# Spectral pairs every fifth step, and the order of two turns in one queue

## The chip, the cores and the metric

The kernel runs on one core of one Trainium2 chip. The metric is the device time of one execution in microseconds (us). A core has five engines that run beside one another and meet at semaphores: TensorE (PE in the profile; its weight loads are PEld), VectorE (DVE), ScalarE (ACT), GpSimd (POOL) and SyncE (SP). SyncE and GpSimd here mostly issue transfers (DMAs), which move data between the core's memory and DRAM on their own. Each engine works through its instructions in the order in which the program was written.

## What is computed

Two operators in a row. The first mixes along the sequence in frequency space: for each of 8 batches of 3008 x 256 numbers a real Fourier transform along the 3008 positions, a product with a complex filter, and the inverse transform. The second is a two-layer perceptron with a PReLU between, on the 24064 rows of 256 that come out.

```python
def _attn_ref(x, filt_r, filt_i):          # x: 8 x 3008 x 256
    X = np.fft.rfft(x, axis=1)
    F = (filt_r + 1j * filt_i)[None, :, :]
    return np.fft.irfft(X * F, n=x.shape[1], axis=1).astype(np.float32)

def _moe_ref(x, w_in, w_out, alpha):       # x: 24064 x 256, w_in: 256 x 2048
    h = x @ w_in
    g = np.maximum(h, 0.0) + alpha * np.minimum(h, 0.0)
    return (g @ w_out).astype(np.float32)
```

## The kernel before

The transform of length 3008 = 47 x 64 is done as matrix products in four stages, each cut into small pieces (class `Fft`, one object for each batch `b`).

- `piece_a` (16 for a batch): one matmul (L168) over the 47 long axis, evicted by `evict` (`on_act`, line 250) into `asb`. After every fourth piece `save_a` (L173) writes a quarter of `asb` to the scratch array `a_dram`; `load_x` then loads the next batch's quarter through GpSimd's queue (L123).
- `turn_a` (L180): four DMAs read `a_dram` back, turned, into `at`. They need the last `save_a` landed.
- `piece_b` (12, called spectral pairs here, two frequencies k1 each): two matmuls (L188) from `at` into a PSUM bank, then two DVE products with the filter, `uu` (L191) and `ww` (L192). `piece_c` (12): four matmuls (L220 reads `uu`, L221 reads `ww`), evicted into `v`.
- `turn_c(q)` (L230): after every third pair four DMAs write a quarter of `v` to `v_dram`. With the last quarter, q = 3, four more (L236) read all of `v_dram` back, turned, into `zt`. These need the writes landed. This is the inverse turn.
- `piece_d` (16): four matmuls (L243) from `zt`, evicted into `yT`, the perceptron's input. Pieces 0 to 3 give the first 752 of a batch's 3008 columns.

`asb`, `at`, `v` and `zt` have one buffer each; the banks `psF` for the pieces two, `uu` and `ww` two each, the output tile `osb` three.

The perceptron runs over blocks of tokens, twelve for each two batches: five of 512, one of 384, six of 512 (`sizes`). A block has 16 steps. In a step j, `up(j)` does two matmuls (L332) into half of `hps`; on odd j the whole of `hps` is evicted by ACT (L337) into `gt`, and DVE does the PReLU with two L340 and one L341. In the same step `prev.down(j)` does a sixteenth of the second product of the block before (L350: four matmuls, or three over the 384 block). When two groups of 128 tokens are complete, ACT evicts them into `osb` (L355) and SyncE stores them (L316).

So there are 768 steps, 96 for each batch, numbered by `step` through the whole run. The Fourier pieces are hung on these steps by a plan written out by hand: `plan_fft(b, a0, ga, ta, b0, gap, d0)` puts `piece_a(i)` on step a0 + ga i, `turn_a` on step ta, `piece_b(kp)` on b0 + gap kp, `piece_c(kp)` three steps later, `turn_c(q)` on b0 + gap (3q + 2) + 4, and `piece_d` from d0 on, the first five on successive steps and the others on every second one. Within a step come `up`, then `down`, then the pieces, those of an earlier batch first. For batches 3 to 7 the arguments are given from p = 96 (b - 1), 96 steps before the batch's own tokens are needed by `up`; batch 2 has p = 96 with a row of its own.

All of `save_a`, `turn_a`, `turn_c` and the stores go through SyncE's one queue, in the order of the steps, and an issue that has to wait holds up the ones behind it. The next batch plans its `piece_a` from p + 42 to p + 72 of the batch at hand, so its `turn_a` falls near the last `turn_c` of that batch.

Of the kernel before, what the change touches and what calls it, by code (L numbers as in the profile page):

```python
# [66 lines left out]
def kernel(  # L67
# [52 lines left out]
    def load_x(b, c):  # L120
        xs = p_x.tile([2 * N1, 8 * D], FP16, name="xs")
        for h in range(2):
            nc.gpsimd.dma_start(out=xs[h * N1 : h * N1 + N1], in_=xrow(b, h, c))  # L123
        return xs
# [236 lines left out]
    def put(step, fn, *args):  # L361
        plan.setdefault(step, []).append((fn, args))

    def plan_fft(b, a0, ga, ta, b0, gap, d0):
        f = Fft(b)
        for i in range(16):
            put(a0 + ga * i, f.piece_a, i, on_act)
        for c in range(4):
            put(a0 + ga * (4 * c + 3), f.save_a, c)
            if b + 1 < NB:  # L370
                put(a0 + ga * (4 * c + 3) + 1,
                    lambda b=b, c=c: xc.update({(b + 1, c): load_x(b + 1, c)}))
        put(ta, f.turn_a, nc.sync)
        for kp in range(12):
            put(b0 + gap * kp, f.piece_b, kp)
            put(b0 + gap * kp + 3, f.piece_c, kp, on_act)
        for q in range(4):
            put(b0 + gap * (3 * q + 2) + 4, f.turn_c, q)
        for i in range(16):
            put(d0 + min(i, 4) + 2 * max(i - 4, 0), f.piece_d, i, on_act)  # L380

    for i in range(4, 16):
        put(i - 4, f0.piece_d, i, both[i % 2])
    plan_fft(1, 10, 1, 26, 40, 3, 91)
    plan_fft(2, 50, 2, 82, 104, 6, 187)
    for b in range(3, NB):
        p = 96 * (b - 1)
        plan_fft(b, p - 54, 2, p - 20, p + 8, 6, p + 91)

    prev = None  # L390
    step = 0
# [43 lines left out]
```

## Time and profile before

| what | value |
|---|---|
| runs shown | 888.08, 890.47, 891.27 us, median 890.47 |
| the profiled execution | 890.82 us |
| its span, first to last instruction | 889.0 us |
| mean granted clock of TensorE | 0.966 |
| ScalarE busy | 587.4 us |
| DMA, mean over the span | 108 GB/s |

A row of the groups by line reads: line, engine, operation, what is written from what, shapes, count; then busy time and mean duration (ns); then the idle time of the engine just before, and what ended it. A row of the timeline has its start, its length, the engine, the line, and in brackets the idle time before it and what ended that. Matmuls are pipelined, so a matmul's length overlaps the next one's; the distance of two starts is what PE spends. A row of waits names who waited for whom: total, times, longest. A row of the windows gives a stretch, its length, then busy time of PE, PEld, DVE, ACT and POOL, and behind these the granted clock, the share of the DMA engines and the rate in GB/s. "SPq" is SyncE's queue of issues; the length there is the time the issuing took.

### The profile page before, as it was taken

What the parts mean: (1) busy time and instruction counts of PE and PEld (TensorE: products, weight loads), DVE (VectorE), ACT (ScalarE), POOL (GpSimd) and SP (SyncE); (2) the same over time, 40 slices, a digit from 0 to 9 for tenths busy, and PEclk for the clock granted to TensorE, in tenths of its full rate; (3) what the DMA queues carried; (4) which work ended last, traced back from release to release, by engine and by line L of the source; (5) the groups of instructions that cost most, each with busy time, mean ns of one, the idle gap of its engine ahead of it and who ended that gap; (6) DMA issues with size and microseconds to landing.
All of it is one profiled execution on the core that took longest, in us unless ns stands there. A gap on an engine that the chain in (4) does not pass through costs nothing.

```text
span 889.0 us, 15377 instructions
## 1 busy us (share of the span) xinstructions
PE 806.8 (91%) x5809; PEld 548.3 (62%) x5809; DVE 612.1 (69%) x1361; ACT 587.4 (66%) x817; POOL 41.3 (5%) x85
## 2 busy tenths in 40 slices
PE   3568899989997999979997999969999899999997
PEld 1234566757664766657664776647666577776665
DVE  2347577668774787748875687748877578877774
ACT  2137667767874768657784768748687576677663
POOL 4102000000000001000010000000000000000000
PEclk9979999989998999989998999989999899999999
DMA  9988916842566136832358224681336422241111
GB/s 213 248 181 172 197 39 134 202 87 56 126 135 158 27 70 131 164 107 49 89 121 184 63 55 94 148 178 31 72 94 129 116 49 54 54 126 31 41 40 52
DMA packets 95378, 95.95 MB, mean 108 GB/s; under 512 B 8312, under 2 KB 85128, under 8 KB 95176
## 3 DMA queue, kind: packets, MB, share of 16 engines
q1 hardware_dynamic: 85448, 78.19, 34.9%
q0 software_dynamic: 8256, 16.00, 12.1%
q10 hardware_dynamic: 1600, 0.79, 0.5%
q8 instruction: 45, 0.74, 0.3%
q14 instruction: 29, 0.24, 0.1%
HBM read 59.55 MB, written 49.81 MB: 123 GB/s over the span
## 4 chain that ended last, share of the span: by engine, by line
PE 81%; DMA 10%; issue 4%; SPq 2%; ACT 2%; POOL 0%; DVE 0%; POOLq 0%; ACTq 0%; DVEq 0%
PE op L350 34%; PE hps L332 34%; PE psF L168 3%; DMA v_dram<-v 3%; PE psF L243 2%; DMA zt<-v_dram 2%; PE psF L220 2%; PE psF L221 2%; PE psF L188 2%; DMA at<-a_dram 2%; DMA a_dram<-asb 2%; DMA xs<-in_x_dram 1%; SPq L230 1%; ACT gt L337 1%; PE hps L168 0%
## 5 line engine op out<-in xcount | busy, mean ns | idle before, releaser
L337 ACT ACTIVATE gt<-hps 128x1024 f16<-128x1024 f32 (+1 forms) x384 | 385.2, 1003 | 149.4 <-PE hps L332 148.1
L332 PE MATMUL hps<-yT,win_s 128*128 128x512 f16 (+1 forms) x1536 | 460.6, 382 | 0.1
L350 PE MATMUL op<-wout_s,gt 128*128 128x256 f16 x3008 | 457.9, 275 | 0.6 <-DVE gt L341 0.6
L350 PEld LDWEIGHTS <-gt 128*128 128x128 f16 x3008 | 296.8, 99 | 195.7 <-issue 8.8
L340 DVE TENSOR_SCALAR m<-gt,alm_s 128x512 f16<-128x512 f16 (+1 forms) x768 | 233.7, 346 | 197.0 <-ACT gt L337 196.5
L341 DVE TENSOR_TENSOR gt<-gt,m 128x1024 f16<-128x1024 f16 (+1 forms) x384 | 261.7, 681 | 21.8
L332 PEld LDWEIGHTS <-win_s 128*128 128x128 f16 x1536 | 146.7, 100 | 31.2 <-issue 5.3
L250 ACT ACTIVATE asb<-psF 96x512 f16<-96x512 f32 x120 | 70.9, 594 | 48.9 <-PE psF L168 48.9
L250 ACT ACTIVATE yT<-psF 128x376 f16<-128x376 f32 x120 | 57.9, 483 | 55.1 <-PE psF L243 54.7
L243 PE MATMUL psF<-wi_s,zt 96*128 96x94 f16 x504 | 45.6, 218 | 40.1 <-DMA zt<-v_dram 38.5
L243 PEld LDWEIGHTS <-zt 96*128 96x128 f16 x512 | 38.6, 106 | 50.5 <-DMA zt<-v_dram 40.2
L191 DVE TENSOR_TENSOR uu<-psF,filt_s 128x512 f16<-128x512 f32 x84 | 57.4, 684 | 5.8 <-PE psF L188 5.8
L355 ACT ACTIVATE osb<-op 128x512 f32<-128x512 f32 x96 | 56.1, 584 | 7.0 <-PE op L350 3.7
L168 PE MATMUL psF<-xs,wf_s 94*96 94x512 f16 x120 | 48.5, 404 | 11.0 <-DMA xs<-in_x_dram 8.9
L192 DVE TENSOR_TENSOR ww<-psF,filts_s 128x512 f16<-128x512 f32 x84 | 57.2, 681 | 0.0
L123 POOL DMA_DIRECT2D xs<-in_x_dram x64 | 32.8, 520 | 475.4 <-PE psF L168 474.3
L250 ACT ACTIVATE v<-psF 128x512 f16<-128x512 f32 x84 | 50.2, 597 | 3.9 <-PE psF L221 3.6
L220 PE MATMUL psF<-uu,twi_s 128*128 128x256 f16 x168 | 41.5, 274 | 0.0
L221 PE MATMUL psF<-ww,twi_s 128*128 128x256 f16 x168 | 41.3, 273 | 0.0
L188 PE MATMUL psF<-at,twf_s 128*128 128x256 f16 x168 | 32.3, 274 | 7.2 <-issue 7.2
L250 ACT ACTIVATE v<-op 128x512 f16<-128x512 f32 x12 | 7.2, 597 | 32.4 <-PE op L221 32.4
L168 PEld LDWEIGHTS <-wf_s 94*96 94x96 f16 x128 | 16.6, 133 | 15.1 <-issue 11.7
(35 smaller groups left out, 134.2 us busy)
## 6 DMA issues: line engine op xcount, KB each, us to landing
out_dram<-osb SPq DMA_DIRECT2D x128, 128.0 KB
a_dram<-asb SPq DMA_DIRECT2D x32, 384.0 KB
v_dram<-v SPq DMA_DIRECT2D x128, 96.0 KB
zt<-v_dram SPq DMA_DIRECT2D x32, 384.0 KB
xs<-in_x_dram POOLq DMA_DIRECT2D x64, 188.0 KB, 5.0
at<-a_dram SPq DMA_DIRECT2D x28, 384.0 KB
twi_s<-c_twi SPq DMA_DIRECT2D x2, 768.0 KB
filts_s<-filt_s SPq DMA_DIRECT2D x2, 768.0 KB
```

Of the source, the lines that this page charges most:

```text
L168: nc.tensor.matmul(ps[0:96], wf1_s, xs[:, o : o + 512], start=True, stop=True)
L191: nc.vector.tensor_mul(uu, px, filt_s[:, 2 * kp : 2 * kp + 2])
L192: nc.vector.tensor_mul(ww, px, filts_s[:, 2 * kp : 2 * kp + 2])
L220: nc.tensor.matmul(pv[:, kh], twi_s[:, k1, 0], uu[:, kh], start=True, stop=False)
L221: nc.tensor.matmul(pv[:, kh], twi_s[:, k1, 1], ww[:, kh], start=False, stop=True)
L243: nc.tensor.matmul(ps[:, m], self.zt[:, 8 * g + 4 * mh + m, dh * 128 : dh * 128 + 128], wi3_s, start=True, stop=True)
L250: nc.scalar.activation(o, i, AF.Copy)
L332: nc.tensor.matmul(self.hps[:, j % 2, 0:tn], win_s[:, kt, j * 128 : (j + 1) * 128], yT[:, kt, self.t0 : self.t0 + tn], start=(kt == 0), st ...
L337: nc.scalar.activation(g[:, :, 0:tn], self.hps[:, :, 0:tn], AF.Copy)
L340: nc.vector.tensor_scalar(m[:, i, 0:tn], g[:, i, 0:tn], 0.0, a, OP.min, OP.mult)
L341: nc.vector.tensor_add(g[:, :, 0:tn], g[:, :, 0:tn], m[:, :, 0:tn])
L350: nc.tensor.matmul(self.op[:, si % 2], self.gts[k][:, 128 * si : 128 * si + 128], wout_s[:, k], start=(k == 0), stop=(k == 15))
```

## The change

Only arguments of `plan_fft` are changed.

```diff
-    plan_fft(1, 10, 1, 26, 40, 3, 91)
-    plan_fft(2, 50, 2, 82, 104, 6, 187)
+    plan_fft(1, 10, 1, 26, 40, 3, 92)
+    plan_fft(2, 50, 2, 86, 104, 5, 187)
     for b in range(3, NB):
         p = 96 * (b - 1)
-        plan_fft(b, p - 54, 2, p - 20, p + 8, 6, p + 91)
+        plan_fft(b, p - 54, 2, p - 22, p + 6, 5, p + 91)
```

In steps counted from p, for batches 3 to 7:

| piece | before | after |
|---|---|---|
| `turn_a` of this batch | p - 20 | p - 22 |
| `turn_a` of the next batch | p + 76 | p + 74 |
| `piece_b` | p + 8, 14, 20 ... 74 | p + 6, 11, 16 ... 61 |
| `piece_c` | p + 11, 17 ... 77 | p + 9, 14 ... 64 |
| `turn_c` 0 to 3 | p + 24, 42, 60, 78 | p + 20, 35, 50, 65 |
| `piece_d` | p + 91 ... 117 | the same |

For batch 2 (p = 96) the pairs start at step 104 with a gap of 5 instead of 6, so `turn_c(3)` is on step 163 instead of 174; its `turn_a` goes from step 82 to 86. Batch 1 keeps all but `piece_d`, which begins on step 92 instead of 91. No instruction is added, removed or changed in size.

## The prediction

> **What bounds the kernel now.** I read the page first, then what TensorE (PE) waits for, then SyncE's queue around one of these waits, then the granted clock behind it.
>
> ```profile
> span 889.0 us, 15377 instructions
> PE 806.8 (91%) x5809; PEld 548.3 (62%) x5809; DVE 612.1 (69%) x1361; ACT 587.4 (66%) x817; POOL 41.3 (5%) x85
> L340 DVE TENSOR_SCALAR m<-gt,alm_s 128x512 f16<-128x512 f16 (+1 forms) x768 | 233.7, 346 | 197.0 <-ACT gt L337 196.5
> L250 ACT ACTIVATE yT<-psF 128x376 f16<-128x376 f32 x120 | 57.9, 483 | 55.1 <-PE psF L243 54.7
> L243 PE MATMUL psF<-wi_s,zt 96*128 96x94 f16 x504 | 45.6, 218 | 40.1 <-DMA zt<-v_dram 38.5
> ```
>
> PE is busy for 806.8 of 889.0 us, so 82.2 us of idle PE are all that a reordering can win. Half of it, 40.1 us, stands before `piece_d` (L243), and 38.5 of that wait for `zt`, which `turn_c(3)` reads back from `v_dram`. One of the six waits is batch 0's, at 62 us, where nothing changes. The waits of PE between 200 and 720 us give the rest in one row:
>
> ```profile
> PE psF L243 <- DMA zt<-v_dram: 30.3, 5, 7.5
> ```
>
> It is the only row of that answer: from 200 to 720 us PE waits for nothing but `zt`, five times, before `piece_d(0)` of batches 2 to 6, 30.3 us in all. Why `zt` is late stands in SyncE's queue, here before batch 4's wait:
>
> ```profile
> 465.68 0.52 SPq L173 DMA_DIRECT2D a_dram<-asb  x1
> 471.19 3.67 SPq L180 DMA_DIRECT2D at<-a_dram  x4
> 474.95 3.86 SPq L230 DMA_DIRECT2D v_dram<-v  x4
> 483.23 1.72 SPq L236 DMA_DIRECT2D zt<-v_dram  x4
> ...
> 487.27 0.50 PE L243 MATMUL psF<-wi_s,zt 96*128 96x94 f16 x4 [6.42 <-DMA zt<-v_dram]
> ```
>
> Batch 5's last `save_a` goes out at 465.68; its `turn_a` (step 76) needs that save landed and leaves at 471.19; batch 4's `turn_c(3)` (step 78) stands behind it, writes `v` from 474.95, and its reads wait for that write until 483.23, landing at 487.27. PE had come to `piece_d` 6.42 us earlier.
>
> The trace also has the order that the change asks for. Batch 1's last turn stands ahead of batch 2's array read, and batch 7's has no array read near it:
>
> ```profile
> 158.16 1.79 SPq L230 DMA_DIRECT2D v_dram<-v  x4
> 162.56 1.72 SPq L236 DMA_DIRECT2D zt<-v_dram  x4
> ...
> 166.76 0.58 SPq L173 DMA_DIRECT2D a_dram<-asb  x1
> 173.99 2.94 SPq L180 DMA_DIRECT2D at<-a_dram  x4
> ...
> 169.74 0.33 PE L243 MATMUL psF<-wi_s,zt 96*128 96x94 f16 x4
> ...
> 788.92 0.33 PE L243 MATMUL psF<-wi_s,zt 96*128 96x94 f16 x4
> ```
>
> From the first write of `v` to the last read of `zt` takes 6.1 us there (158.16 to 164.28), and `piece_d(0)` carries no wait for either batch, though batch 1 has only 14 steps between `turn_c(3)` (77) and `piece_d(0)` (91).
>
> **What the change removes.** Steps below are counted from the batch's own p. For batches 3 to 6, `turn_c(3)` moves from 78 to 65, `turn_a` of the next batch from 76 to 74, `piece_d(0)` stays at 91: the turn is 9 steps ahead of the array read and 26 steps, instead of 13, ahead of its reader. At 0.87 us a step or more (rows below) that is over 22 us; the turn needs 6.1 us and a landing of 4.0 us (483.23 to 487.27). Batch 2's turn goes to 67. So I take off all five waits, 30.3 us. What is late next: the following `save_a` (72) finds SyncE free again at about 72 (my estimate: an eviction after step 65 and the 6.1 us), and `turn_a` still waits for that save to land. It keeps its 28 steps (74 to 102, before 76 to 104), over 24 us, ahead of its first reader, which has no wait among the rows of this stretch; a few us of delay there stay hidden. The stores of steps 71 and 79 come some us later; `osb` has three buffers and one is filled every eighth step, so I cost that at nothing.
>
> The clock is the second part. Each wait makes the granted clock fall to half, and work goes on at half speed after PE resumes. The windows view gives the ten us after each of the five waits:
>
> ```profile
> 277.47:287.47 10.00, 10.00 (x69) 6.47 (x70) 3.23 (x8) 6.20 (x10) 0.00 (x0) 0.75 0.51 138
> 382.70:392.70 10.00, 10.00 (x73) 6.98 (x74) 3.08 (x9) 6.05 (x11) 0.00 (x0) 0.72 0.53 151
> 487.27:497.27 10.00, 10.00 (x77) 6.75 (x78) 3.93 (x9) 6.71 (x11) 0.00 (x0) 0.83 0.51 144
> 592.82:602.82 10.00, 10.00 (x78) 7.01 (x79) 3.73 (x10) 6.97 (x12) 0.00 (x0) 0.82 0.57 157
> 693.77:703.77 10.00, 10.00 (x68) 6.48 (x69) 3.23 (x8) 6.20 (x10) 0.00 (x0) 0.74 0.50 136
> ...
> 117.00:160.00 43.00, 40.96 (x287) 28.05 (x285) 34.71 (x73) 32.26 (x47) 3.02 (x6) 1.00 0.49 111
> ```
>
> PE is busy throughout; the third number from the end is the clock. Work lost is 10 us times what is missing to 1: 2.5 + 2.8 + 1.7 + 1.8 + 2.6 = 11.4 us. This goes with the waits. Together 30.3 + 11.4 = 41.7 us. The last row is for later: 2.0 us of short waits (43.00 less 40.96) left the clock at 1.00.
>
> [...]
>
> **What the change adds.** The number of pairs is the same; they come every 5 steps instead of 6. Before, every pair of batches 2 to 7 stood on an even step. Now every second one, six of the twelve in each batch, stands on an odd step, and odd steps are those on which `up` emits the whole ACT and VectorE (DVE) group (L337, L340, L341). DVE works in order, so on an odd step the two products of `piece_b` queue behind that same step's group. Batch 1 has such a pair at step 61; an even one is batch 4's last, step 74:
>
> ```profile
> 136.93 0.60 PE L332 MATMUL hps<-yT,win_s 128*128 128x512 f16 x2
> 137.80 0.27 PE L220 MATMUL psF<-uu,twi_s 128*128 128x256 f16 x1
> 138.24 0.38 PE L188 MATMUL psF<-at,twf_s 128*128 128x256 f16 x2
> 138.46 0.59 PE L332 MATMUL hps<-yT,win_s 128*128 128x512 f16 x2
> 139.32 0.69 DVE L341 TENSOR_TENSOR gt<-gt,m 128x1024 f16<-128x1024 f16 x1
> 139.32 0.38 PE L168 MATMUL psF<-xs,wf_s 94*96 94x512 f16 x1
> 139.54 0.60 PE L332 MATMUL hps<-yT,win_s 128*128 128x512 f16 x2
> 140.53 0.68 DVE L192 TENSOR_TENSOR ww<-psF,filts_s 128x512 f16<-128x512 f32 x1
> 141.39 0.27 PE L221 MATMUL psF<-ww,twi_s 128*128 128x256 f16 x1
> ...
> 464.40 0.59 PE L332 MATMUL hps<-yT,win_s 128*128 128x512 f16 x2
> 467.13 0.68 DVE L192 TENSOR_TENSOR ww<-psF,filts_s 128x512 f16<-128x512 f32 x1
> 468.20 0.27 PE L221 MATMUL psF<-ww,twi_s 128*128 128x256 f16 x1
> ```
>
> From the start of its step, `ww` is done after 4.28 us on the odd step (136.93 to 141.21) and after 3.41 us on the even one (464.40 to 467.81). L221 of `piece_c`, three steps on, came after 4.46 and 3.80 us: 0.18 and 0.39 us to spare. The odd pair of batch 1 was saved by its longer steps, since with a gap of 3 its own step also held another `piece_c`, 0.44 us (137.80 to 138.24). At a gap of 5 that is gone.
>
> Terms: `up` and `down` 0.87 us (138.46 to 139.32 and a hundredth), `piece_b` 0.22 (138.24 to 138.46), `piece_a` 0.22 (139.32 to 139.54), and these rows for `piece_d`, 0.16 (405.41 to 405.57), and for a step over a 384-token `down`, 0.76 (401.76 to 402.52):
>
> ```profile
> 401.76 0.60 PE L332 MATMUL hps<-yT,win_s 128*128 128x512 f16 x2
> 402.52 0.38 PE L188 MATMUL psF<-at,twf_s 128*128 128x256 f16 x2
> ...
> 405.41 0.33 PE L243 MATMUL psF<-wi_s,zt 96*128 96x94 f16 x4
> 405.57 0.27 PE L220 MATMUL psF<-uu,twi_s 128*128 128x256 f16 x1
> ```
>
> `ww` is usable at 4.28 + 0.04 = 4.32 us (0.04 is my estimate of the handover). L221 reaches it after three steps, an `up`, a `down` and one L220 of 0.11 us (a quarter of the 0.44):
>
> - step 31: 0.87 + 0.22 + 3 x 0.87 + 0.11 = 3.81, wait 0.51
> - step 21, with a `piece_d`: 3.97, wait 0.35
> - steps 41, 51, 61, with one `piece_a`: 4.03, wait 0.29 each; batch 7 has no `piece_a` behind it, 0.51 each
> - step 11, two `piece_d`: 4.13, wait 0.19 for odd batches; for even ones, over the short `down`, 3.69 and 0.63
> - batch 2, pairs from 104: 0.52, 0.51, 0.51, then 0.29 three times
>
> Sums: 2.4 (batch 2), 1.9, 2.4, 1.9, 2.4, 2.6 (batch 7): 13.6 us. Behind a waiting L221 stands all of PE's queue, and PE has no idle time in this stretch to absorb it. The waits are as short as those of the 117 to 160 us row, so they should not lower the clock.
>
> [...]
>
> Two small terms. Batch 1's `piece_d(3)` moves to step 95, right ahead of step 96, whose `up` reads it: PE waits for the eviction, 0.48 us (L250), and for what ACT still has before it, 0.5 to 1.5 us by my estimate. It is hidden by PE's wait for `at` eight steps later:
>
> ```profile
> 184.37 0.59 PE L188 MATMUL psF<-at,twf_s 128*128 128x256 f16 x2 [3.05 <-issue]
> ```
>
> That wait stays, because `turn_a` of batch 2, at step 86 instead of 82, was held until 173.99 by the landing of its save anyhow; without it the 0.5 to 1.5 us would count.
>
> **Sum.** 890.82 (the profiled execution) - 41.7 + 13.6 = 862.7, say **863 us**. The median of the runs, 890.47, is 0.35 lower, which changes nothing.
>
> **The rivals.**
>
> 1. No new waits: the odd pairs fit as they did in batch 1. 890.8 - 41.7 = 849. For it speaks that batch 1 shows none; against it the missing 0.44 us. 18 in 100.
> 2. The new waits are larger: an eviction ahead of L337 (0.48 us, L250) delays the group. At 36 pairs and up to 0.48 us more each, up to 17 us: 871 to 880. 12 in 100.
> 3. The change doesn't do what it says: `zt` or `at` is late all the same, because the moved reads share the engines with a save and an `x` load. Each wait left costs 6 us and 2.3 us of clock; with most left, 885 to 895. Batches 1 and 7 speak against it. 6 in 100.
> 4. Slower: DVE falls a whole group behind. If `ww` comes after a second L340 and L341 group (2 x 0.35 + 0.69 = 1.39 us), 36 pairs lose 0.38 + 1.39 us, 64 us, and the result is 913; it turns slower once a pair waits 41.7 / 36 = 1.16 us. From 22 to 41 DVE has 5 groups and 2 pairs (four products of 0.68) in 10 steps, 7.0 + 2.7 = 9.7 us against PE's 10.0 (8.7 + 2 x 0.66), which speaks against a lasting lag. 4 in 100.
>
> The forecast, 855 to 871, has the remaining 60. The range that leaves no more than 2 in 10 out reaches from just below rival 1 to the end of rival 2: **847 to 880**. A measurement of this kernel tells about 0.5% (4.5 us) from no change: faster by more 0.92, within 0.03, slower by more 0.05.
>
> **What would show it.** The row of `zt` waits between 200 and 720 us gone, and PEclk 1.00 around each `piece_d(0)`; in SyncE's queue `zt` reads ahead of `at` reads; new rows "PE psF L221 <- DVE ww" or L220, some 36 of 0.2 to 0.6 us; 3 us left before batch 2's first L188. No waits on `ww` would make me wrong by 14 us; a remaining `zt` wait, or waits for `at` of batches 3 to 7, would break the first term.

## The result, and the profile after

| | before | after |
|---|---|---|
| median of the runs | 890.87 us (888.08 to 892.26) | 860.42 us (858.72 to 863.19) |
| ratio, with its 95% interval | | 0.9665 (0.9627 to 0.9703) |
| the profiled execution | 890.82 us | 863.19 us |

The kernel is faster by 30 us by the medians. The profiled execution of the changed kernel is the slowest of its four runs, and shows 27.6 us; 863 us had been forecast, with 28.1 us as the sum.

These are the rows of the page after that answer to those shown of before, with the row of L221, which has come up in the list:

```profile
span 861.4 us, 15404 instructions
PE 799.4 (93%) x5809; PEld 541.7 (63%) x5809; DVE 612.9 (71%) x1361; ACT 586.6 (68%) x817; POOL 41.4 (5%) x85
L243 PE MATMUL psF<-wi_s,zt 96*128 96x94 f16 x504 | 42.7, 207 | 10.8 <-DMA zt<-v_dram 9.0
L221 PE MATMUL psF<-ww,twi_s 128*128 128x256 f16 x168 | 41.1, 272 | 6.2 <-DVE ww L192 3.5
```

The idle time before L243 falls from 40.1 to 10.8 us, and the 9.0 us left of `zt` are batch 0's wait at the start. TensorE's waits from 190 to 700 us, where before there was only `zt`, are now these:

```profile
PE psF L221 <- DVE ww L192: 2.2, 8, 0.3
PE psF L220 <- ACT yT L250: 0.5, 2, 0.2
PE psF L220 <- DVE ww L192: 0.4, 1, 0.4
```

SyncE's queue around batch 3's inverse turn, and the first `piece_d` that reads it:

```profile
351.93 3.67 SPq L230 DMA_DIRECT2D v_dram<-v  x4
359.12 1.78 SPq L236 DMA_DIRECT2D zt<-v_dram  x4
362.73 0.62 SPq L173 DMA_DIRECT2D a_dram<-asb  x1
370.32 2.43 SPq L180 DMA_DIRECT2D at<-a_dram  x4
...
372.67 0.33 PE L243 MATMUL psF<-wi_s,zt 96*128 96x94 f16 x4
```

The reads of `zt` are issued by 360.90, ahead of the array read, and TensorE comes to them at 372.67 without a bracket: it waited for nothing. The windows view around that place shows TensorE busy throughout and the clock (third number from the end) at 1.00:

```profile
370.00:380.00 10.00, 10.00 (x96) 7.63 (x95) 6.42 (x18) 8.04 (x15) 0.00 (x0) 1.00 1.02 181
```

**A wait that the profile half hides.** The rows for `ww` say 3.5 + 0.4 us, and the sum needed 13.6. The timeline after tells why; here is batch 2's pair on step 129 (odd), whose `piece_c` is on step 132:

```profile
213.81 0.59 PE L332 MATMUL hps<-yT,win_s 128*128 128x512 f16 x2
214.68 0.38 PE L188 MATMUL psF<-at,twf_s 128*128 128x256 f16 x2
216.15 0.69 DVE L341 TENSOR_TENSOR gt<-gt,m 128x1024 f16<-128x1024 f16 x1
216.75 0.68 DVE L191 TENSOR_TENSOR uu<-psF,filt_s 128x512 f16<-128x512 f32 x1
217.36 0.68 DVE L192 TENSOR_TENSOR ww<-psF,filts_s 128x512 f16<-128x512 f32 x1
217.50 0.27 PE L220 MATMUL psF<-uu,twi_s 128*128 128x256 f16 x1
218.09 0.27 PE L221 MATMUL psF<-ww,twi_s 128*128 128x256 f16 x1 [0.32 <-DVE ww L192]
218.20 0.27 PE L220 MATMUL psF<-uu,twi_s 128*128 128x256 f16 x1
```

The step starts at 213.81, and `ww` ends at 218.04, 4.23 us later. L221 starts at 218.09. In an undisturbed `piece_c` it starts 0.11 us after L220 (218.09 to 218.20 is such a distance), so it should have come at 217.61: 0.48 us late. The bracket says 0.32, because L220 is drawn 0.27 us long and so covers 0.16 us of the wait. A wait of 0.3 us is covered so far that it gets no row at all. So these waits must be read from the distances of starts: L220 to the first L221, and the end of `down` to the first L220. Over all pairs of the trace after they add up to 2.5, 2.0, 2.4, 1.9, 2.4 and 2.5 us for batches 2 to 7, together 13.7 us. The same reading of batches 3 to 7 before gives 0.0.

**A fair place to measure from.** The start-up differs by some us from run to run, so the traces are compared below from batch 2's first L188 to the end. The windows view gives the first ten us and the whole stretch, before and after:

```profile
184.37:194.37 10.00, 10.00 (x61) 6.21 (x62) 5.29 (x12) 6.03 (x9) 0.00 (x0) 0.70 0.12 32
184.37:889.00 704.63, 668.95 (x4911) 464.28 (x4911) 506.33 (x1140) 489.07 (x673) 16.09 (x32) 0.97 0.39 90
```
```profile
186.55:196.55 10.00, 9.59 (x66) 6.23 (x67) 6.49 (x14) 7.17 (x11) 0.00 (x0) 0.83 0.11 28
186.55:861.40 674.85, 662.08 (x4911) 458.07 (x4911) 507.29 (x1140) 488.24 (x673) 16.28 (x32) 1.00 0.40 94
```

The stretch is 704.63 us before and 674.85 after. Both start in a clock dip left by the wait in front of that L188, which cost 3.0 us before (10 x 0.30) and 1.7 us after. Without these the two are 701.6 and 673.2: 28.4 us gained.

### The profile page after: what moved, and what is told of

The parts are those of the page before. It is cut to its first block, busy times and chain, and to the rows that moved or that the text cites. A ratio compares the mean times of both kernels' runs of the same rounds, so it can differ in the third digit from the quotient of the medians.

```text
span 861.4 us, 15404 instructions
## 1 busy us (share of the span) xinstructions
PE 799.4 (93%) x5809; PEld 541.7 (63%) x5809; DVE 612.9 (71%) x1361; ACT 586.6 (68%) x817; POOL 41.4 (5%) x85
## 4 chain that ended last, share of the span: by engine, by line
PE 70%; DVE 13%; ACT 7%; DMA 6%; issue 2%; SPq 1%; POOL 0%; ACTq 0%; DVEq 0%; POOLq 0%
PE hps L332 29%; PE op L350 28%; ACT gt L337 6%; DVE gt L341 4%; DVE m L340 4%; PE psF L168 3%; DVE ww L192 3%; DVE uu L191 3%; PE psF L221 2%; DMA at<-a_dram 2%; PE psF L243 2%; DMA a_dram<-asb 2%; PE psF L220 1%; DMA xs<-in_x_dram 1%; PE psF L188 1%
## 5 line engine op out<-in xcount | busy, mean ns | idle before, releaser
L337 ACT ACTIVATE gt<-hps 128x1024 f16<-128x1024 f32 (+1 forms) x384 | 385.1, 1003 | 134.6 <-PE hps L332 134.1
L332 PE MATMUL hps<-yT,win_s 128*128 128x512 f16 (+1 forms) x1536 | 454.3, 377 | 1.1 <-ACT yT L250 1.0
L350 PE MATMUL op<-wout_s,gt 128*128 128x256 f16 x3008 | 453.3, 273 | 0.6 <-DVE gt L341 0.6
L250 ACT ACTIVATE asb<-psF 96x512 f16<-96x512 f32 x120 | 70.7, 593 | 40.2 <-PE psF L168 40.2
L250 ACT ACTIVATE v<-psF 128x512 f16<-128x512 f32 x84 | 50.2, 598 | 34.9 <-PE psF L221 34.9
L250 ACT ACTIVATE yT<-psF 128x376 f16<-128x376 f32 x120 | 58.1, 484 | 20.9 <-PE psF L243 20.7
L243 PE MATMUL psF<-wi_s,zt 96*128 96x94 f16 x504 | 42.7, 207 | 10.8 <-DMA zt<-v_dram 9.0
L243 PEld LDWEIGHTS <-zt 96*128 96x128 f16 x512 | 36.3, 100 | 18.9 <-DMA zt<-v_dram 9.3
L221 PE MATMUL psF<-ww,twi_s 128*128 128x256 f16 x168 | 41.1, 272 | 6.2 <-DVE ww L192 3.5
L220 PE MATMUL psF<-uu,twi_s 128*128 128x256 f16 x168 | 42.9, 272 | 1.1 <-ACT yT L250 0.5
L188 PE MATMUL psF<-at,twf_s 128*128 128x256 f16 x168 | 32.3, 274 | 8.1 <-issue 4.5
L220 PEld LDWEIGHTS <-twi_s 128*128 128x128 f16 x192 | 19.0, 99 | 18.0 <-issue 13.2
L250 ACT ACTIVATE v<-op 128x512 f16<-128x512 f32 x12 | 7.2, 597 | 32.4 <-PE op L221 32.4
```

The source lines that it names most:

```text
L220: nc.tensor.matmul(pv[:, kh], twi_s[:, k1, 0], uu[:, kh], start=True, stop=False)
L221: nc.tensor.matmul(pv[:, kh], twi_s[:, k1, 1], ww[:, kh], start=False, stop=True)
L243: nc.tensor.matmul(ps[:, m], self.zt[:, 8 * g + 4 * mh + m, dh * 128 : dh * 128 + 128], wi3_s, start=True, stop=True)
L250: nc.scalar.activation(o, i, AF.Copy)
L332: nc.tensor.matmul(self.hps[:, j % 2, 0:tn], win_s[:, kt, j * 128 : (j + 1) * 128], yT[:, kt, self.t0 : self.t0 + tn], start=(kt == 0), st ...
L337: nc.scalar.activation(g[:, :, 0:tn], self.hps[:, :, 0:tn], AF.Copy)
```

## The experiments

**Theory:** the gain is the five waits for `zt` and the half clock behind them, about 41.7 us, because of where the inverse turn stands; about 14 us of it are given back because every second pair now stands on an odd step. **Rivals:** the gain is from the pairs ending earlier, not from the turn; the new waits are from the density of pairs, not from their parity; the order in the queue decides, and not the distance. Times are medians of four runs; before had medians of 888.78 us beside the first four kernels and 887.0 us beside the last three.

### The turn put back, the pairs left

```diff
-            put(b0 + gap * (3 * q + 2) + 4, f.turn_c, q)
+            put(96 * (b - 1) + 78 if q == 3 and b > 1
+                else b0 + gap * (3 * q + 2) + 4, f.turn_c, q)
...
-        plan_fft(b, p - 54, 2, p - 22, p + 6, 5, p + 91)
+        plan_fft(b, p - 54, 2, p - 20, p + 6, 5, p + 91)
```

> Pairs every fifth step as changed, but turn_c(3) put back to p + 78, behind the next batch's turn_a at p + 76. Theory (the gain is the turn's place): the five waits for zt, about 30 us, and the half clock behind them, about 11 us, come back on top of the waits for ww: 900 to 905 us. Rival (the gain is that the last pairs end earlier, wherever the turn stands): about 860 us.

Measured: 904.86 us (902.84 to 906.67), 1.018 times before (1.0148 to 1.0212): slower, though 2% lies inside the interval. The first row is TensorE's wait for `zt` from 100 us on, then one of the five in the timeline, with the queue that makes it:

```profile
PE psF L243 <- DMA zt<-v_dram: 33.6, 5, 7.9
...
370.62 3.33 SPq L180 DMA_DIRECT2D at<-a_dram  x4
373.99 3.65 SPq L230 DMA_DIRECT2D v_dram<-v  x4
382.15 1.72 SPq L236 DMA_DIRECT2D zt<-v_dram  x4
...
385.96 0.50 PE L243 MATMUL psF<-wi_s,zt 96*128 96x94 f16 x4 [7.68 <-DMA zt<-v_dram]
```

All five are back. From batch 2's first L188 (184.46, no dip) to the end (902.2) are 717.7 us, 44.6 more than the changed kernel's 673.2; 33.6 of them are the waits, and 11.0 are left for the clock, against 11.4 in the forecast; the clock in the ten us behind each of the five waits (0.83, 0.75, 0.79, 0.74 and 0.85) gives 10.4. Read from the starts, `piece_c` waits the same 13.7 us as in the changed kernel, so nothing of the 44.6 is on that side. Pairs that end earlier bring nothing by themselves: with the turn late they cost.

### Only the order changed

```diff
-        plan_fft(b, p - 54, 2, p - 20, p + 8, 6, p + 91)
+        plan_fft(b, p - 54, 2, p - 14, p + 8, 6, p + 91)
```

> The pairs as before, every sixth step on even steps; only the next batch's turn_a is moved, from p + 76 to p + 82, behind turn_c(3) at p + 78. Theory (order in the queue decides): zt takes some 6 us to be issued and 4 us to land after step 78, 13 steps of 0.87 us are 11.3 us, so the five waits shrink to 0 to 1 us each, PEclk stays 1.00 and no wait for ww appears: 848 to 855 us. Rival (the distance of 26 steps is what counts, not the order): waits of 3 us and more stay and the clock still falls, 870 to 890 us.

Measured: 846.81 us (846.70 to 847.16), 0.9525 (0.9506 to 0.9545). The median is just under the 848 to 855 us expected. This is one argument of the kernel before: the pairs stay where they were, and only the array read steps behind the inverse turn. SyncE's queue, the first `piece_d` behind it, and the whole stretch from 190 to 700 us:

```profile
355.02 1.80 SPq L230 DMA_DIRECT2D v_dram<-v  x4
358.50 1.72 SPq L236 DMA_DIRECT2D zt<-v_dram  x4
362.66 5.68 SPq L180 DMA_DIRECT2D at<-a_dram  x4
...
365.03 0.33 PE L243 MATMUL psF<-wi_s,zt 96*128 96x94 f16 x4
...
190.00:700.00 510.00, 509.78 (x3830) 356.22 (x3827) 399.21 (x895) 389.07 (x549) 16.04 (x32) 1.00 0.48 108
```

From 355.02 to 365.03 are 10.0 us, and `piece_d` doesn't wait: 13 steps are enough once nothing stands ahead. TensorE is busy for 509.78 of 510 us at full clock, so in this stretch there is nothing more for a reordering to win. From batch 2's first L188 (184.93, no dip) to the end (845.1) are 660.1 us, 41.5 less than before's 701.6: the waits and the clock behind them, 41.7 us in the forecast, measured without the odd pairs.

### Every pair on an even step

```diff
-            put(b0 + gap * kp, f.piece_b, kp)
-            put(b0 + gap * kp + 3, f.piece_c, kp, on_act)
+            s = b0 + gap * kp - (gap * kp % 2 if gap == 5 else 0)
+            put(s, f.piece_b, kp)
+            put(s + 3, f.piece_c, kp, on_act)
```

> The changed kernel with every odd-step pair moved one step earlier, so that pairs stand on p + 6, 10, 16, 20, 26 ...; mean distance still 5. Theory (parity: on an odd step the products queue behind the same step's PReLU group): the 14 us of waits for ww go, 845 to 849 us. Rival (density: DVE is too loaded with a pair every fifth step): the waits stay, 858 to 863 us.

Measured: 849.19 us (846.65 to 850.66), 0.9549 (0.9522 to 0.9575). The median is just above the 845 to 849 us expected and far from the rival's 858. The density is that of the changed kernel, and the waits are gone. The stretch, then a pair:

```profile
190.00:700.00 510.00, 510.00 (x3836) 356.65 (x3835) 403.06 (x897) 390.42 (x550) 16.03 (x32) 1.00 0.47 109
...
215.56 0.38 PE L188 MATMUL psF<-at,twf_s 128*128 128x256 f16 x2
217.37 0.68 DVE L192 TENSOR_TENSOR ww<-psF,filts_s 128x512 f16<-128x512 f32 x1
218.49 0.27 PE L221 MATMUL psF<-ww,twi_s 128*128 128x256 f16 x1
```

`ww` ends 0.44 us before its reader. From batch 2's first L188 (184.88, no dip) to the end (844.9) are 660.0 us, 13.2 less than the changed kernel's 673.2, beside the 13.7 counted from its starts.

### All pairs on odd steps, the rest as before

```diff
-    plan_fft(2, 50, 2, 82, 104, 6, 187)
+    plan_fft(2, 50, 2, 82, 105, 6, 187)
...
-        plan_fft(b, p - 54, 2, p - 20, p + 8, 6, p + 91)
+        plan_fft(b, p - 54, 2, p - 20, p + 9, 6, p + 91)
```

> The kernel before with all pairs one step later, on odd steps, distance 6, turn order as before. Theory (parity): all 72 pairs of batches 2 to 7 wait for ww, 0.2 to 0.6 us each, some 26 us, with the five waits for zt kept: 912 to 922 us. Rival (density): no new waits, 889 to 893 us.

Measured: 920.27 us (916.05 to 921.13), 1.0342 (1.0309 to 1.0374). TensorE's waits from 186 us on:

```profile
PE psF L243 <- DMA zt<-v_dram: 31.4, 6, 6.6
PE psF L221 <- DVE ww L192: 10.8, 34, 0.3
```

One step later, at the old distance of 6, costs 31 us by the medians. Read from the starts, `piece_c` waits about 28 us in the six batches; 34 of the 72 pairs are long enough to get a row of L221. From the first L188 (183.33) to the end (914.3) are 731.0 us, 29.4 more than before's 701.6. One thing was not expected: a sixth wait for `zt`, 2.6 us before batch 7's `piece_d(0)` (812.49), whose turn also comes a step later; the other five come to 28.8 us, so the waits for `zt` are 1.1 us above before's 30.3 in all. Parity makes the waits for `ww`, not density.

### One step more for the reader

```diff
-            put(b0 + gap * kp + 3, f.piece_c, kp, on_act)
+            put(b0 + gap * kp + (4 if gap == 5 else 3), f.piece_c, kp, on_act)
...
-            put(b0 + gap * (3 * q + 2) + 4, f.turn_c, q)
+            put(b0 + gap * (3 * q + 2) + (5 if gap == 5 else 4), f.turn_c, q)
```

> The changed kernel with piece_c four steps after its piece_b instead of three for batches 2 to 7 (turn_c one step later too); half of the pairs still stand on odd steps. Theory (ww is done 4.3 us after its step's start, and the reader comes 0.2 to 0.6 us too early): one more step of 0.76 us or more covers every wait, so 845 to 850 us and no row of waits for ww. Rival (odd steps cost TensorE time of their own, for instance in the two psF banks): 855 to 863 us, with waits moved to L168 or L188.

Measured: 850.42 us (847.42 to 853.58), 0.9590 (0.9547 to 0.9634). The median is 0.4 us above the 845 to 850 expected. Odd pairs are harmless when `piece_c` comes four steps later. What remains from 186 us on has no `ww` in it; 0.9 us are the rival's kind, waits of `piece_a` for a `psF` bank:

```profile
PE psF L188 <- issue: 1.8, 1, 1.8
PE psF L168 <- ACT v L250: 0.9, 5, 0.2
PE op L350 <- DVE gt L341: 0.6, 1, 0.6
```

### Batch 2's pairs six steps later, on even steps

Against the even-step version:

```diff
-    plan_fft(1, 10, 1, 26, 40, 3, 92)
-    plan_fft(2, 50, 2, 86, 104, 5, 187)
+    plan_fft(1, 10, 1, 26, 40, 3, 91)
+    plan_fft(2, 50, 2, 86, 110, 5, 187)
```

> The even-step version with batch 2's pairs six steps later (110 instead of 104) and batch 1's piece_d back at 91. Theory: the wait for at before batch 2's first pair (3 to 6 us) goes with its clock dip, and the 1.0 us at step 96 goes: 839 to 845 us. Rival (that wait is not worth what it shows, since other work fills it later): no change against the even-step version.

Measured: 842.92 us (841.56 to 844.84), 0.9505 (0.9476 to 0.9533): the fastest of all, though its interval overlaps that of the order change alone. Against the even-step version it is 6.3 us by the medians. The trace of that version shows 3.3 us of the waits meant here, 2.34 in front of batch 2's first L188 and 0.99 at step 96, and no clock dip behind them; the rest isn't accounted for. Batch 2's first L188 has no wait in front:

```profile
187.44 0.38 PE L188 MATMUL psF<-at,twf_s 128*128 128x256 f16 x2
```

### The old order with the new distance

Against the even-step version:

```diff
-        plan_fft(b, p - 54, 2, p - 22, p + 6, 5, p + 91)
+        plan_fft(b, p - 66, 2, p - 32, p + 6, 5, p + 91)
```

> The even-step version with piece_a and its turns twelve and turn_a ten steps earlier for batches 3 to 7, so that the next batch's turn_a (p + 64) stands again ahead of turn_c(3) (p + 65), while the turn keeps 26 steps to its reader. If the distance is enough, whatever the order: about 16 us behind turn_a against 22 us of room, no waits for zt, 846 to 853 us. If the order in the queue is what decides: waits of some us and the clock dips come back, 865 us and more.

Measured: 851.12 us (848.07 to 851.57), 0.9588 (0.9553 to 0.9622). The array read is ahead of the inverse turn again, and `piece_d` does not wait:

```profile
348.49 2.44 SPq L180 DMA_DIRECT2D at<-a_dram  x4
350.97 3.56 SPq L230 DMA_DIRECT2D v_dram<-v  x4
360.64 1.73 SPq L236 DMA_DIRECT2D zt<-v_dram  x4
...
368.29 0.33 PE L243 MATMUL psF<-wi_s,zt 96*128 96x94 f16 x4
```

From the write of `v` to the last read issued takes 11.4 us behind the array read (350.97 to 362.37), and 5.2 us ahead of it in the kernel with only the order changed (355.02 to 360.22). So either is enough here: the place ahead of the array read with 13 steps, or 26 steps behind it. The changed kernel gives it both, and pays for the distance with the odd steps.

## Why the prediction was right

- **The waits for `zt`, 30.3 us.** All five are gone, and come back, as 33.6 us, when the turn is put back. With only the order changed they and the clock dips go too, and 41.5 us are won where 41.7 stood.
- **The clock behind them, 11.4 us.** With the turn put back 11.0 us are left beside the waits. The dips before are each 6.83 us long at a clock of 0.50, but all five begin inside the wait, 1.26 to 3.43 us before TensorE resumes, and only the part behind it slows work. These 11 us came out of TensorE's busy time, so the 82.2 us of idle TensorE that the prediction starts from were not all that a reordering could win.
- **The odd pairs, 13.6 us.** Counted 13.7; the even-step version gains 13.2 of them. The terms hold one by one as well: 0.48 us where 0.51 stood, 0.31 where 0.29 and 0.35 stood. The handover of 0.04 us was near (218.04 to 218.09). What the step got wrong is how the waits would show: it named some 36 new rows, and 13 are there, since the drawn length of the matmul before covers up to 0.16 us of each. And in batches 4 and 6, 0.4 us of the wait at the pair on p + 11 stands before the first L220 and is ended by ACT's eviction of a `piece_d`, which frees a `psF` bank (the row "PE psF L220 <- ACT yT L250" above); the sum had put all of it on `ww`.
- **Step 96 and batch 2's `at`.** The wait of 0.5 to 1.5 us is there, 0.99, and ends at a wait for `at` of 3.62 us, so it was hidden as said. The row before, "<-issue", names no releaser; the row after names `at`, as the prediction took it:

```profile
175.30 0.38 PE L332 MATMUL hps<-yT,win_s 128*128 128x512 f16 x1 [0.99 <-ACT yT L250]
...
186.55 0.38 PE L188 MATMUL psF<-at,twf_s 128*128 128x256 f16 x2 [3.62 <-DMA at<-a_dram]
```

- **The stores and the next `save_a`, at nothing.** No row of the stretch from 190 to 700 us names `osb` or `at`.
- **The rivals.** "No new waits" would have been 849 us, which is what the even-step version gives; "larger waits" did not come, because no eviction delayed L337 by much: in all 36 odd pairs `ww` ended 4.22 to 4.37 us after its step's start, against 4.28 in the forecast. That also answers the fourth rival, a DVE that falls a whole group behind. The third was a late `zt` or `at`, and TensorE waits for neither in batches 3 to 7.

That the median lies 2.6 us under the forecast is not in these terms. The profiled execution, 863.19 us, had its first L188 of batch 2 at 186.55, 2.2 us later than before's. Two kernels of the experiments, the one with the turn put back and the one with every pair on an even step, have the same plan up to there and came to it at 184.46 and 184.88, so some 2 us of it can be the start-up of that one execution; the other runs of the changed kernel left no trace, and the point stays open.

## What to carry to other kernels

A transfer chain that was late at its reader was mended here by its place in the queue and, in another run, by its distance; the cheaper of the two should be tried alone: one argument that moved the array read gave 42 us, the whole change 30. When work is put on another step of a two-step rhythm, look at what else its engine does on that step: the same products, one step over, cost 28 us. A short wait behind a matmul was covered in part here (0.16 of 0.48 us), or wholly, by that matmul's drawn length of 0.27 us, and then doesn't appear as idle time; read the distances of starts.

## What was not expected of the hardware

The clock fell or did not fall after waits of nearly the same length. In the ten us after the wait in front of batch 2's first pair it was 0.70 after 3.05 us before the change and 0.83 after 3.62 us with it, but in the kernel with only the order changed a wait of 3.32 us left it whole:

```profile
184.93 0.38 PE L188 MATMUL psF<-at,twf_s 128*128 128x256 f16 x2 [3.32 <-DMA at<-a_dram]
...
184.93:194.93 10.00, 10.00 (x85) 7.12 (x86) 8.11 (x18) 8.37 (x14) 0.00 (x0) 1.00 0.17 46
```

The times at which the granted clock changes are in the traces, and they tell these cases apart. In those of the kernel before and of the changed one it is either whole or half, and within each of the two all its changes lie a whole number of steps of 3.41 us apart; where these steps fall differs between the two (a change at 183.47 us before, at 187.41 us after). Cut into steps of this length, the windows view gives this for the kernel before, for only the order changed, and for the old order with the new distance:

```profile
180.06:183.47 3.41, 1.26 (x13) 0.71 (x10) 2.02 (x5) 1.40 (x2) 0.00 (x0) 1.00 1.21 203
183.47:190.29 6.82, 5.92 (x28) 3.41 (x29) 2.69 (x6) 3.18 (x5) 0.00 (x0) 0.50 0.17 57
```
```profile
179.94:183.35 3.41, 1.67 (x14) 0.95 (x12) 2.43 (x6) 1.56 (x3) 0.00 (x0) 1.00 1.24 191
183.35:186.76 3.41, 1.83 (x16) 1.30 (x17) 1.29 (x2) 0.98 (x2) 0.00 (x0) 1.00 0.52 154
```
```profile
183.35:186.76 3.41, 1.15 (x12) 0.74 (x11) 1.78 (x4) 0.59 (x3) 0.00 (x0) 1.00 0.77 190
186.76:190.17 3.41, 3.41 (x17) 1.94 (x15) 2.13 (x5) 2.30 (x4) 0.00 (x0) 0.50 0.00 0
```

In the first, TensorE is idle for 2.15 of the 3.41 us (3.41 less 1.26), and the clock is half from there on. In the second the longer wait of 3.32 us is split over two steps, 1.74 and 1.58 us, and the clock stays whole. In the third a wait of only 2.26 us lies in one step, and the clock falls. The traces of the kernel before and of the changed one agree with this from 100 us to the end: at whole clock, each of their 11 steps in which TensorE was idle for 2.00 us or more was followed by half clock, and none of those with 1.78 us or less. So in these cases the fall went not with the length of the wait but with the idle time within one step. The start-up is not in this count, and no run here shows why the clock falls.
